# Splitting the first loads of an MLP forward-and-backward kernel, and starting the first product on half of its columns

## The chip, the cores and the metric

The kernel runs on one core of a Trainium2 chip. The metric is device time in microseconds (us) of one execution. A profiled execution's span is about 1.9 us shorter than its time (320.1 against 321.97 us for the kernel before). Times inside a trace count from the start of the span.

## The reference

```python
# x: 2048 x 640, w1: 640 x 1536, w2: 1536 x 640, grad_out: 2048 x 640, all bf16
h   = silu(x @ w1)
out = h @ w2
# returned: out and the gradients of x, w1 and w2 for grad_out
```

## The kernel before

Everything is 128 x 128 weights times up to 512 moving columns on TensorE. Rows of x are handled in four chunks of 512 (four tiles of 128). For each chunk the kernel makes h transposed (`h_group`, 12 groups of 5 matmuls), the output, and the gradients that go back to x; at the end come the two weight gradients. The first chunk of x is transposed on TensorE, since nothing else can run yet; later chunks come transposed by DMA.

The parts that the change touches, with cuts marked:

```python
NWARM = 36
warm = cpool.tile([P, P], dt_in, name="warm")
nc.vector.memset(warm[:], 0.0)
nc.scalar.activation(warm_a[:], warm[:, 0:1], ACT.Silu)      # loads the table early
for i in range(NWARM):                                       # L97: warm-up, result unused
    nc.tensor.matmul(wp[:, 0:P], lhsT=warm[:], rhs=warm[:], start=True, stop=True)
# ... cut
def pe_xT(c, halves):                                        # called as pe_xT(0, 1)
    # ... cut
        for dt_ in range(DT):
            # ... cut: the bank tp is allocated
            for j in range(nst):                             # L125: 4 transposes into one bank (st = j here)
                nc.tensor.transpose(tp[:, j, :], x_nat[:, st, dt_*P:(dt_+1)*P], ident[:])
            # copy the bank to xT: VectorE (L128) for even dt_, ScalarE (L130) for odd

FH = FC // 2                                                 # 256
nc.sync.dma_start(out=x_nat[:, 0:STC, :], in_=x_v[:, 0:STC, :])         # 640 KB
nc.sync.dma_start(out=w1_nat[:, :, 0:FH], in_=w1_v[:, :, 0:FH])         # 320 KB
nc.sync.dma_start(out=w1_nat[:, :, FH:FC], in_=w1_v[:, :, FH:FC])       # 320 KB
# ... cut: rest of w1, w2, transposed loads
xT_next = pe_xT(0, 1)

def h_group(ft, xT, aT, ghT):
    hp = ps_h.tile([P, SC], FP32, name="hp")
    for dt_ in range(DT):                                    # L151: 5 matmuls, 512 columns
        nc.tensor.matmul(hp[:], lhsT=w1_nat[:, dt_, ft*P:(ft+1)*P], rhs=xT[:, dt_, :],
                         start=(dt_ == 0), stop=(dt_ == DT - 1))
    # ... cut: Silu and Tanh on ScalarE, two VectorE instructions

# chunk c, cut:
if c == 1:
    for j in range(0, ST, STC):                              # 4 transfers, used at the very end
        nc.sync.dma_start(out=go_nat[:, j:j + STC, :], in_=go_v[:, j:j + STC, :])
if c == 0:
    for ft in range(FT):
        h_group(ft, xT, aT, ghT)
    # ... cut: store, then sd_phase (L186: output matmuls), ...
```

## Time and profile before

| | before |
|---|---|
| time, median of 3 (of 6 with the comparison runs) | 321.95 us (321.89) |
| span of the profiled execution | 320.1 us |
| x (640 KB) complete | 5.25 us |
| first w1 piece (256 columns) complete | 6.36 us |
| first h matmul | 6.42 us |
| first output matmul | 19.38 us |
| from the start of the last matmul (317.21) to the end ("the tail" below) | 2.90 us |

The two landings are the last of sixteen partial landings: the trace's landing records have sixteen for each of these loads. The chain of waits of the kernel before, its first 21 us (start, duration, what it was):

```profile
0.74 4.51 DMA x_nat<-in_x_dram
5.25 0.05 issue
5.30 1.29 PE tp L125 x20
6.59 12.95 PE hp L151 x60
19.54 1.51 PE hp L186 x7
```

After the load of x there is only TensorE work. The groups view says the same for the whole run (busy us, mean ns; then idle time before them):

```profile
L151 PE MATMUL hp<-xT,w_nat 128*128 128x512 bf16 x240 | 56.9, 379 | 0.0
...
L186 PE MATMUL hp<-aT,w_nat 128*128 128x512 bf16 x240 | 52.5, 379 | 0.0
```

The mean of 379 ns is the length of one pipelined matmul; the pace is 12.95 us for 60, or 216 ns each. The timeline of the kernel before (start, duration, group, count) shows the head:

```profile
0.74 0.43 SPq L134 DMA_DIRECT2D x_nat<-in_x_dram  x1
...
0.99 4.02 PE L97 MATMUL wp<-warm 128*128 128x128 bf16 x36 [0.99 <-DVE warm L92]
...
1.23 0.49 SPq L135 DMA_DIRECT2D w_nat<-in_w_dram  x1
...
5.30 1.29 PE L125 MATMUL tp<-ident,x_nat 128*128 128x128 bf16 x20 [0.28 <-DMA x_nat<-in_x_dram]
...
6.42 13.12 PE L151 MATMUL hp<-xT,w_nat 128*128 128x512 bf16 x60
...
19.38 6.85 PE L186 MATMUL hp<-aT,w_nat 128*128 128x512 bf16 x31
```

How to read a pace here: a group lasts from its first start to its last end. For the warm-up, (4.02 - 0.31) / 35 = 106 ns from start to start; for the transposes, (1.29 - 0.22) / 19 = 56 ns (0.31 and 0.22 us are one instruction's length). Both stream 128 columns: the array ran at half clock in the warm-up and at full clock in the transposes.

### The profile page before, as it was taken

The page shows a single profiled execution, that of the slowest core. Times are in us where ns is not written, and L with a number is a line of the kernel's source. Part 1 is how long each engine was busy: PE and PEld are TensorE (multiplying, and loading weights), DVE is VectorE, ACT ScalarE, POOL GpSimd, SP SyncE. Part 2 cuts the span into 40 slices and gives each one's busy share as a digit, 9 for nine tenths or more (in the row PEclk, how much of TensorE's full clock was granted, in tenths as well). Part 3 has the DMA queues.
Part 4 walks back from the last instruction along what each step waited for, and adds up shares of the span by engine and source line. Part 5 has one row for each costly group of instructions (what it writes and reads, how often), then busy time and mean ns, then how long its engine had stood idle before and what let it go on. Part 6 is the DMA issues. An engine that isn't in the chain of part 4 may idle for free.

```text
span 320.1 us, 3590 instructions
## 1 busy us (share of the span) xinstructions
PE 316.2 (99%) x1512; PEld 146.7 (46%) x1512; DVE 101.9 (32%) x179; ACT 78.3 (24%) x140; POOL 0.7 (0%) x6
## 2 busy tenths in 40 slices
PE   8999999999999999999999999999999999999996
PEld 7444444444444444444444444444444444444443
DVE  1871551477510087710147751000000100001001
ACT  3960001555201255401154520110100001001100
POOL 0000000000000000000000000000000000000000
DMA  8999999999999855291635079809999999994111
GB/s 232 314 194 190 252 222 274 341 263 309 262 286 296 227 180 151 69 324 63 175 109 146 2 247 269 224 16 301 260 241 242 269 209 342 238 293 166 52 37 47
DMA packets 149200, 66.69 MB, mean 208 GB/s; under 512 B 112576, under 2 KB 149184, under 8 KB 149184
## 3 DMA queue, kind: packets, MB, share of 16 engines
q1 hardware_dynamic: 149184, 66.46, 81.8%
q8 instruction: 12, 0.20, 0.3%
q14 instruction: 4, 0.03, 0.0%
HBM read 9.18 MB, written 28.97 MB: 119 GB/s over the span
## 4 chain that ended last, share of the span: by engine, by line
PE 98%; DMA 1%; DVE 0%; issue 0%; DVEq 0%
PE hp L186 32%; PE hp L151 16%; PE hp L276 16%; PE hp L170 16%; PE hp L324 15%; DMA x_nat<-in_x_dram 1%; PE hp L306 1%; PE tp L125 0%; DVE g_2364 L317 0%; DVEq L317 0%
## 5 line engine op out<-in xcount | busy, mean ns | idle before, releaser
L151 PE MATMUL hp<-xT,w_nat 128*128 128x512 bf16 x240 | 56.9, 379 | 0.0
L170 PE MATMUL hp<-goT,w2T 128*128 128x512 bf16 x240 | 56.9, 379 | 0.0
L186 PE MATMUL hp<-aT,w_nat 128*128 128x512 bf16 x240 | 52.5, 379 | 0.0
L186 PE MATMUL hp<-ghT,w1T 128*128 128x512 bf16 x240 | 52.5, 379 | 0.0
L276 PE MATMUL hp<-a_blk,go_nat 128*128 128x512 bf16 x240 | 52.0, 379 | 0.0
L324 PE MATMUL hp<-gh_blk,x_nat 128*128 128x512 bf16 x224 | 48.5, 379 | 0.0
L194 ACT ACTIVATE oT<-hp 128x512 bf16<-128x512 f32 x24 | 14.3, 597 | 110.0 <-PE hp L186 110.0
L186 PEld LDWEIGHTS <-w_nat 128*128 128x128 bf16 x240 | 23.5, 98 | 28.3
L170 PEld LDWEIGHTS <-w2T 128*128 128x128 bf16 x240 | 23.5, 98 | 28.3
L276 PEld LDWEIGHTS <-go_nat 128*128 128x128 bf16 x240 | 23.5, 98 | 28.3
L186 PEld LDWEIGHTS <-w1T 128*128 128x128 bf16 x240 | 23.4, 98 | 28.4
L158 ACT ACTIVATE aT<-hp 128x512 bf16<-128x512 f32 x48 | 28.7, 598 | 31.1 <-PE hp L151 31.1
L151 PEld LDWEIGHTS <-w_nat 128*128 128x128 bf16 x240 | 23.4, 98 | 28.1
L196 DVE CAST oT<-hp 128x512 bf16<-128x512 f32 x16 | 11.1, 692 | 78.0 <-PE hp L186 78.0
L177 DVE SCALAR_TENSOR_TENSOR ghT<-ghT,hp 128x512 bf16<-128x512 bf16 x48 | 32.5, 683 | 7.3 <-PE hp L170 7.3
L324 PEld LDWEIGHTS <-x_nat 128*128 128x128 bf16 x224 | 21.9, 98 | 26.4
L163 DVE SCALAR_TENSOR_TENSOR ghT<-aT,v 128x512 bf16<-128x512 bf16 x48 | 33.0, 688 | 0.6
L162 DVE TENSOR_SCALAR v<-t 128x512 bf16<-128x512 f32 x48 | 20.5, 427 | 28.5 <-ACT t L160 28.5
L160 ACT ACTIVATE t<-hp 128x512 f32<-128x512 f32 x48 | 28.4, 591 | 0.0
L286 DVE CAST g2T<-hp 128x512 bf16<-128x512 f32 x7 | 4.8, 692 | 46.1 <-PE hp L276 46.1
L284 ACT ACTIVATE g2T<-hp 128x512 bf16<-128x512 f32 x8 | 4.8, 598 | 47.0 <-PE hp L276 47.0
L97 PE MATMUL wp<-warm 128*128 128x128 bf16 x36 | 4.0, 313 | 1.0 <-DVE warm L92 1.0
(32 smaller groups left out, 27.0 us busy)
## 6 DMA issues: line engine op xcount, KB each, us to landing
aT_scr<-aT SPq DMA_DIRECT2D x4, 1536.0 KB, 6.2
ghT_scr<-ghT SPq DMA_DIRECT2D x4, 1536.0 KB, 10.1
out_dram<-o_sb SPq DMA_DIRECT2D x8, 640.0 KB, 3.4
x_nat<-in_x_dram SPq DMA_DIRECT2D x4, 640.0 KB, 4.7
oT_scr<-oT SPq DMA_DIRECT2D x4, 640.0 KB, 4.3
go_nat<-in_grad_out_dram SPq DMA_DIRECT2D x4, 640.0 KB, 7.1
gxT_scr<-oT SPq DMA_DIRECT2D x4, 640.0 KB, 4.7
w_nat<-in_w_dram SPq DMA_DIRECT2D x2, 960.0 KB, 11.3
```

What stands on the lines that cost most here:

```text
L151: nc.tensor.matmul(hp[:], lhsT=w1_nat[:, dt_, ft * P:(ft + 1) * P], rhs=xT[:, dt_, :], start=(dt_ == 0), stop=(dt_ == DT - 1),)
L158: nc.scalar.activation(aT[:, ft, :], hp[:], ACT.Silu)
L160: nc.scalar.activation(t[:], hp[:], ACT.Tanh, scale=0.5)
L162: nc.vector.tensor_scalar(out=v[:], in0=t[:], scalar1=-0.5, scalar2=0.5, op0=ALU.mult, op1=ALU.add)
L163: nc.vector.scalar_tensor_tensor(out=ghT[:, ft, :], in0=aT[:, ft, :], scalar=1.0, in1=v[:], op0=ALU.subtract, op1=ALU.mult)
L170: nc.tensor.matmul(gp[:], lhsT=w2T[:, dt_, ft * P:(ft + 1) * P], rhs=goT[:, dt_, :], start=(dt_ == 0), stop=(dt_ == DT - 1),)
L177: nc.vector.scalar_tensor_tensor(out=ghT[:, ft, :], in0=ghT[:, ft, :], scalar=1.0, in1=gp[:], op0=ALU.add, op1=ALU.mult)
L186: nc.tensor.matmul(op_[:], lhsT=w_all[:, ft, dt_ * P:(dt_ + 1) * P], rhs=rhs_all[:, ft, :], start=(ft == 0), stop=(ft == FT - 1),)
L194: nc.scalar.activation(oT[:, dt_, :], op_[:], ACT.Copy)
L196: nc.vector.tensor_copy(out=oT[:, dt_, :], in_=op_[:])
L276: nc.tensor.matmul(gp[:], lhsT=go_nat[:, st, dt_ * P:(dt_ + 1) * P], rhs=a_blk[:, st, :], start=(st == 0), stop=(st == ST - 1),)
L324: nc.tensor.matmul(gp[:], lhsT=x_nat[:, st, dt_ * P:(dt_ + 1) * P], rhs=gh_blk[:, st, :], start=(st == 0), stop=(st == ST - 1),)
```

## The change

The intent: h needs x and w1, and half of the rows of the chunk are enough for a start. So two tiles of x and 256 columns of w1 come first (640 KB instead of 960), the second tile through ScalarE's queue. The first two h groups start on 256 columns; tiles 2 and 3 are transposed between them; then the groups are completed. The warm-up reads a constant and so starts earlier, with fewer matmuls, and four filler matmuls follow the first transposes to keep TensorE busy.

```diff
-    NWARM = 36
+    NWARM = 26
+    NFILL = 4
@@
-        warm = cpool.tile([P, P], dt_in, name="warm")
-        nc.vector.memset(warm[:], 0.0)
+        warm = nc.const_aps.tensor(1.0, (P, P), dt_in)
@@
-        nc.sync.dma_start(out=x_nat[:, 0:STC, :], in_=x_v[:, 0:STC, :])
-        nc.sync.dma_start(out=w1_nat[:, :, 0:FH], in_=w1_v[:, :, 0:FH])
-        nc.sync.dma_start(out=w1_nat[:, :, FH:FC], in_=w1_v[:, :, FH:FC])
+        load_x_tile(nc.sync, 0)
+        load_x_tile(nc.scalar, 1)
+        load_w1(0, FH)
+        load_x_tile(nc.sync, 2)
+        load_x_tile(nc.sync, 3)
+        load_w1(FH, FC)
 ... (ScalarE's early Silu moves behind its load)
-        xT_next = pe_xT(0, 1)
+        def pe_x_tile(xT, st):        # 3 transposes, VectorE copy; 2 transposes, ScalarE copy
+            ...
+        for st in range(2):
+            pe_x_tile(xT_next, st)
+        for i in range(NFILL):
+            nc.tensor.matmul(wp[:, 0:P], lhsT=ident[:], rhs=x_nat[:, 1, 0:P], start=True, stop=True)
 ... (h_mm: the five matmuls of a group on columns lo to hi)
             if c == 0:
-                for ft in range(FT):
+                hps = []
+                for ft in range(2):
+                    hp = ps_h.tile([P, SC], FP32, name="hp")
+                    h_mm(hp, ft, xT, 0, XL)          # XL = 256
+                    hps.append(hp)
+                    pe_x_tile(xT, 2 + ft)
+                for ft in range(2):
+                    h_mm(hps[ft], ft, xT, XL, SC)
+                    h_group(ft, xT, aT, ghT, hps[ft])
+                for ft in range(2, FT):
                     h_group(ft, xT, aT, ghT)
```

More of the change, by code (lines that the diff above doesn't have):

```diff
@@ L89 @@
         opool = mctx.enter_context(tc.tile_pool(name="opool", bufs=2))
-        warm = cpool.tile([P, P], dt_in, name="warm")
-        nc.vector.memset(warm[:], 0.0)
+        warm = nc.const_aps.tensor(1.0, (P, P), dt_in)
         warm_a = cpool.tile([P, 1], FP32, name="warm_a")
-        nc.scalar.activation(warm_a[:], warm[:, 0:1], ACT.Silu)
         wp = ps_h.tile([P, SC], FP32, name="wp", tag="hp")
         for i in range(NWARM):
-            nc.tensor.matmul(wp[:, 0:P], lhsT=warm[:], rhs=warm[:], start=True, stop=True)
+            nc.tensor.matmul(wp[:, 0:P], lhsT=warm, rhs=warm, start=True, stop=True)
         ident = cpool.tile([P, P], dt_in, name="ident")
@@ L115, in load_goT, with load_w1, load_x_tile @@
             return goT
-        def pe_xT(c, halves):
-            xT = xpool.tile([P, DT, SC], dt_in, name="xT")
-            nst = STC // halves
-            for hh in range(halves):
-                for dt_ in range(DT):
-                    tp = ps_h.tile([P, nst, P], dt_in, name="tp", tag="hp")
-                    for j in range(nst):
-                        st = c * STC + hh * nst + j
-                        nc.tensor.transpose(tp[:, j, :], x_nat[:, st, dt_ * P:(dt_ + 1) * P], ident[:])
-                    dst = xT[:, dt_, hh * nst * P:(hh + 1) * nst * P]
-                    if dt_ % 2 == 0:
-                        nc.vector.tensor_copy(out=dst, in_=tp[:].rearrange("p j q -> p (j q)"))
-                    else:
-                        nc.scalar.copy(out=dst, in_=tp[:].rearrange("p j q -> p (j q)"))
-            return xT
-        FH = FC // 2
-        nc.sync.dma_start(out=x_nat[:, 0:STC, :], in_=x_v[:, 0:STC, :])
-        nc.sync.dma_start(out=w1_nat[:, :, 0:FH], in_=w1_v[:, :, 0:FH])
-        nc.sync.dma_start(out=w1_nat[:, :, FH:FC], in_=w1_v[:, :, FH:FC])
+        FH = FC // 2
+        XL = SC // 2
+        xT_next = xpool.tile([P, DT, SC], dt_in, name="xT")
+        def load_w1(lo, hi):
+            nc.sync.dma_start(out=w1_nat[:, :, lo:hi], in_=w1_v[:, :, lo:hi])
+        def load_x_tile(eng, st):
+            eng.dma_start(out=x_nat[:, st, :], in_=x_v[:, st, :])
+        load_x_tile(nc.sync, 0)
[4 more added lines that the diff above has]
+        load_w1(FH, FC)
         for fc in range(1, NFC):
-            nc.sync.dma_start(out=w1_nat[:, :, fc * FC:(fc + 1) * FC], in_=w1_v[:, :, fc * FC:(fc + 1) * FC])
+            load_w1(fc * FC, (fc + 1) * FC)
+        nc.scalar.activation(warm_a[:], warm[:, 0:1], ACT.Silu)
         for hf in range(2):
@@ L144, with h_mm @@
         nc.sync.dma_start_transpose(out=w1T[:], in_=w1[:, :])
-        xT_next = pe_xT(0, 1)
-        def h_group(ft, xT, aT, ghT):
-            hp = ps_h.tile([P, SC], FP32, name="hp")
+        DS = 3
+        def pe_x_tile(xT, st):
+            for lo, hi, copy in ((0, DS, nc.vector.tensor_copy), (DS, DT, nc.scalar.copy)):
+                tp = ps_h.tile([P, hi - lo, P], dt_in, name="tp", tag="hp")
+                for dt_ in range(lo, hi):
+                    nc.tensor.transpose(tp[:, dt_ - lo, :], x_nat[:, st, dt_ * P:(dt_ + 1) * P], ident[:])
+                copy(out=xT[:, lo:hi, st * P:(st + 1) * P], in_=tp[:])
+        for st in range(2):
+            pe_x_tile(xT_next, st)
+        for i in range(NFILL):
+            nc.tensor.matmul(
+                wp[:, 0:P], lhsT=ident[:], rhs=x_nat[:, 1, 0:P], start=True, stop=True
+            )
+        def h_mm(hp, ft, xT, lo, hi):
             for dt_ in range(DT):
                 nc.tensor.matmul(
-                    hp[:],
+                    hp[:, lo:hi],
                     lhsT=w1_nat[:, dt_, ft * P:(ft + 1) * P],
-                    rhs=xT[:, dt_, :],
+                    rhs=xT[:, dt_, lo:hi],
                     start=(dt_ == 0),
@@ L157, in h_group @@
                 )
+        def h_group(ft, xT, aT, ghT, hp=None):
+            if hp is None:
+                hp = ps_h.tile([P, SC], FP32, name="hp")
+                h_mm(hp, ft, xT, 0, SC)
             nc.scalar.activation(aT[:, ft, :], hp[:], ACT.Silu)
@@ L216 @@
             if c == 0:
-                for ft in range(FT):
+                hps = []
+                for ft in range(2):
+                    hp = ps_h.tile([P, SC], FP32, name="hp")
+                    h_mm(hp, ft, xT, 0, XL)
[5 more added lines that the diff above has]
+                for ft in range(2, FT):
                     h_group(ft, xT, aT, ghT)
```

## The prediction

> **What bounds the kernel now.** The chain of waits is TensorE matmuls for 98% of the 320.1 us span. Only its head is anything else: 4.51 us from the issue of the x load (0.74) until its last part lands (5.25), then 20 transposes (1.29 us). From 6.4 us on TensorE never idles (groups: idle 0.0 for the big matmul lines; 60 matmuls take 12.95 us, 216 ns each). So only the first 6.4 us can be shortened, and what is saved there should reach the end undiminished.
>
> In the DMA landings x (640 KB) is complete at 5.25, the first 256 columns of w1 (320 KB) at 6.36, the next 256 at 7.45. The first h matmul starts at 6.42: transposes and w1 piece end together, so both have to move.
>
> **What changes.**
> 1. Before the first h matmul 640 KB must land instead of 960. In the DMA records 655,000 bytes had moved by 4.36 us, 983,000 by 5.30; landings trailed by 0.9 to 1.0 us. Estimate: x tiles 0 and 1 land at 4.0 to 4.4, the w1 piece at 5.2. The second issuing queue saves little: the Trainium skill ("DMA: Bandwidth & Descriptors", Issuing engines are not separate DMA queues) says both run on the same 16 engines. The first h matmul then starts near 5.2, 1.2 us earlier.
> 2. Given back: ten transposes now come after that start (10 x 56 ns = 0.56 us). Half-width matmuls cost nearly nothing more (0.03 us). And a new wait: the upper halves need the copies of tile 3. The old first copy began 0.43 us after the first transpose and took 0.43; with three transposes and 384 columns I estimate 0.77 from first transpose to first upper-half matmul, of which transposes fill 0.29: a stall of about 0.48 us. Sum: about 1.1 us.
> 3. Net: 0.1 to 0.2 us earlier at the output matmuls, which started at 19.38.
>
> Not critical: later loads (w1 columns 256 to 511 needed near 8.4, landing about 7.4), activations (first Silu near 8.2 instead of 7.71; the twelfth result is needed only 2.4 us into the output matmuls).
>
> 4. Clock. Warm-up matmuls are 106 ns apart until 4.7, transposes from 5.30 on 56 ns: the clock doubled between. The Trainium skill ("TensorE: Matmul & The Clock Gate", Part 1) puts this at about 4 us of sustained activity, judged in a free-running window of 3.4 us. The new warm-up starts 0.25 us earlier, but 26 matmuls run out near 3.5; a gap, short transposes and four fillers follow. Most likely the clock is up by 5.2; if it comes a window later, 3.4 us of h at half rate cost up to 1.7 us. I give that 1 in 5.
>
> **Prediction: 321.7 us**, 0.25 under the 321.95 measured; range 320.9 to 322.7. Chances: faster by over 2% 0.01, within 2% 0.98, slower 0.01.
>
> **What would show each step right or wrong** (new profile): first h matmul near 5.2, released by the landing of the w1 piece; transposes of tiles 2 and 3 not waiting for DMA; an idle of about 0.5 us before the first upper-half matmul, released by the VectorE copy; first half-width matmuls about 110 ns apart (215 if the clock is down); output matmuls starting at 19.2 to 19.3; no idle afterwards.
>
> **What would make it wrong.** The w1 piece landing by 4.8 (if the slow first microsecond of the x load, about 120 GB/s against 330 to 400 later, is a limit of one queue that two lift) would gain another 0.4; a late clock would turn the gain into a loss near 1.5; x tiles 2 or 3 landing after 5.8 and 6.6 would stall the interleaved transposes.

## More of the kernel before

One more view mattered, and I had not looked at it before predicting: what SyncE's queue waits for in the last 5 us (total us, times, longest).

```profile
SPq L363 <- DMA out_dram<-g_2364: 0.5, 1, 0.5
...
SPq L363 <- DMA out_dram<-g_2344: 0.3, 1, 0.3
```

The last two stores are waited for one after the other, g_2364 being the very last.

## The result, and the profile after

| | before | after |
|---|---|---|
| time, median of 6 | 321.89 us (321.7 to 322.4) | 322.5 us (322.1 to 323.04) |
| span of the profiled execution | 320.1 | 321.1 |
| tiles 0 and 1 of x complete | 5.25 (all four) | 3.62 and 3.80 |
| first w1 piece complete | 6.36 | 6.04 (15 of 16 parts by 4.94) |
| first h matmul | 6.42 | 6.08 |
| first output matmul | 19.38 | 20.13 |
| last matmul's start to the end (the tail) | 2.90 | 3.18 |

The ratio is 1.0018, 95% interval 1.0004 to 1.0032: same at 2%, and slower by a fifth of a per cent.

The chain of waits after, first 21 us:

```profile
0.74 0.39 SPq L124
...
1.19 4.84 DMA w_nat<-in_w_dram
...
6.08 0.72 PE hp L160 x5
6.80 0.28 PE tp L148 x5
7.08 0.55 PE hp L160 x5
7.63 0.18 PE tp L148 x3
...
7.83 0.37 DVE xT L149
...
8.25 1.47 PE hp L160 x11
```

Left out are stretches of 0.02 to 0.06 us of "issue". The load that ends last is now w1's, and a VectorE copy (7.83) has entered the chain. The timeline after:

```profile
0.74 0.40 ACTq L124 DMA_DIRECT2D x_nat<-in_x_dram  x1
...
1.19 0.41 SPq L121 DMA_DIRECT2D w_nat<-in_w_dram  x1
...
3.67 1.25 PE L148 MATMUL tp<-ident,x_nat 128*128 128x128 bf16 x10
...
4.71 0.58 PE L154 MATMUL wp<-x_nat,ident 128*128 128x128 bf16 x4
...
6.08 0.72 PE L160 MATMUL hp<-xT,w_nat 128*128 128x256 bf16 x5 [0.80 <-DMA w_nat<-in_w_dram]
...
6.64 0.44 PE L148 MATMUL tp<-ident,x_nat 128*128 128x128 bf16 x5
...
7.47 0.44 PE L148 MATMUL tp<-ident,x_nat 128*128 128x128 bf16 x5
...
8.25 12.04 PE L160 MATMUL hp<-xT,w_nat 128*128 128x256 bf16 x59 [0.34 <-DVE xT L149]
...
20.13 6.21 PE L200 MATMUL hp<-aT,w_nat 128*128 128x512 bf16 x27
```

The last transpose of tile 3 started at 7.69 and the next matmul at 8.25, where 56 ns would have done: a stall of 0.50 us. The fillers are still 106 ns apart (half clock, until 5.03); the transposes at 6.64 are 56 ns apart. From first h matmul to first output matmul it is 14.04 us (20.126 - 6.084 in the records), against 12.95 before (19.376 - 6.423): 1.09 us given back. And at the end, SyncE's queue waits:

```profile
SPq L386 <- DMA out_dram<-g_2375: 1.1, 1, 1.1
```

Only one store is waited for now, the very last one, and for all of the time.

### The profile page after: what moved, and what is told of

It reads as the page before. It is cut to its first block, busy times and chain, and to the rows that moved or that the text cites. A ratio compares the mean times of both kernels' runs of the same rounds, so it can differ in the third digit from the quotient of the medians.

```text
span 321.1 us, 3575 instructions
## 1 busy us (share of the span) xinstructions
PE 314.7 (98%) x1487; PEld 147.5 (46%) x1516; DVE 101.8 (32%) x179; ACT 78.2 (24%) x142; POOL 0.7 (0%) x6
## 3 DMA queue, kind: packets, MB, share of 16 engines
HBM read 9.18 MB, written 28.97 MB: 119 GB/s over the span
## 4 chain that ended last, share of the span: by engine, by line
PE 97%; DMA 2%; issue 1%; DVE 0%; SPq 0%; DVEq 0%
PE hp L200 32%; PE hp L160 16%; PE hp L184 16%; PE hp L299 16%; PE hp L347 15%; DMA w_nat<-in_w_dram 2%; PE hp L329 1%; PE tp L148 0%; SPq L124 0%; DVE xT L149 0%; DVE g_2375 L340 0%; DVEq L340 0%
## 5 line engine op out<-in xcount | busy, mean ns | idle before, releaser
L160 PE MATMUL hp<-xT,w_nat 128*128 128x512 bf16 (+1 forms) x243 | 56.9, 370 | 1.5 <-DMA w_nat<-in_w_dram 0.8
L160 PEld LDWEIGHTS <-w_nat 128*128 128x128 bf16 x250 | 24.4, 98 | 28.5 <-DMA w_nat<-in_w_dram 1.0
L200 PEld LDWEIGHTS <-w_nat 128*128 128x128 bf16 x240 | 23.5, 98 | 28.3
L356 ACT ACTIVATE g_2149<-hp 128x512 bf16<-128x512 f32 x1 | 0.6, 597 | 13.5 <-DMA out_dram<-g_2086 13.5
```

Of the source, the lines that this page charges most:

```text
L160: nc.tensor.matmul(hp[:, lo:hi], lhsT=w1_nat[:, dt_, ft * P:(ft + 1) * P], rhs=xT[:, dt_, lo:hi], start=(dt_ == 0), stop=(dt_ == DT - 1),)
L200: nc.tensor.matmul(op_[:], lhsT=w_all[:, ft, dt_ * P:(dt_ + 1) * P], rhs=rhs_all[:, ft, :], start=(ft == 0), stop=(ft == FT - 1),)
```

## The experiments

The changed kernel's six times fell in two groups (322.1 to 322.2, 322.8 to 323.0), so single traces could mislead. My theory after the first trace was a straggling part of the w1 load (S) against a fixed late landing (F); rivals for the rest were a late clock (C), and for the end another order of final waits (K).

### The changed kernel again

No edit.

> The changed kernel once more, unchanged, for a second trace and five more times. In the first trace of it one of the sixteen landings of the first w1 piece came at 6.04 us, 1.1 us after the fifteenth (4.94), and its six times fell in two groups (322.1 to 322.2 and 322.8 to 323.0). Theory S (a straggling transfer that comes and goes): two groups again; if the profiled run is one of the quick ones, the w1 piece is complete by about 5.0 to 5.3, the first h matmul starts then, and the output matmuls at about 19.1 to 19.4. Rival F (the late landing is a fixed property of the new load order): complete at about 6.0 again, output matmuls at about 20.1, median 322.5 again.

Measured: 322.31 us median (321.94 to 322.49), ratio 1.0013 (1.0001 to 1.0025). In this trace the w1 piece was complete at 4.98, the first h matmul started at 5.03, the first output matmul at 19.07. The timeline:

```profile
3.95 0.73 PE L148 MATMUL tp<-ident,x_nat 128*128 128x128 bf16 x10 [0.30 <-DMA x_nat<-in_x_dram]
4.52 0.39 PE L154 MATMUL wp<-x_nat,ident 128*128 128x128 bf16 x4
5.03 0.72 PE L160 MATMUL hp<-xT,w_nat 128*128 128x256 bf16 x5
...
7.19 2.98 PE L160 MATMUL hp<-xT,w_nat 128*128 128x256 bf16 x18 [0.34 <-DVE xT L149]
```

S holds for this piece, and F falls; but the two groups that I expected did not come back, for the five times (321.94, 322.10, 322.31, 322.47, 322.49) spread without a gap. The way from first h to first output matmul is again 14.04 us, and the tail again 3.17. Note the clock: the same ten transposes and four fillers took 0.73 and 0.39 us here, 1.25 and 0.58 in the first trace. In this execution the clock had doubled by 3.95; in the other it had not by 5.03. Note also that although TensorE ended 0.31 us earlier than in the kernel before, the span is the same 320.1 us.

### One queue

```diff
-        load_x_tile(nc.scalar, 1)
+        load_x_tile(nc.sync, 1)
```

> x tile 1 is issued by SyncE as tile 0 is, so nothing is issued by ScalarE. If the second queue causes the late last landing of the w1 piece (a transfer of one engine pushed behind), the sixteen landings lie within about 0.8 us again, as before the change, the first h matmul starts near 5.3 to 5.5 and the time falls by about 0.6 us against the slow group of the change (322.0 or so). If the second queue helps (it spread the first microsecond's slow transfers over two queues: tiles 0 and 1 landed at 3.6 and 3.8 where I had estimated 4.0 to 4.4), tile 1 lands about 0.4 us later and the w1 piece too, with the straggler still there: 322.5 to 323.

Measured: 322.82 us (322.66 to 322.98), ratio 1.0031 (1.0019 to 1.0043), slower than the change. Two of sixteen parts of the w1 piece straggled (5.95 and 5.97 after 5.09), so the second queue is not what causes stragglers. My second case had tile 1 land about 0.4 us later than with two queues (3.80 in the first trace); it landed earlier, at 3.50, and tile 0 at 2.98 instead of 3.62. So for the tiles of x the second queue was no help; what moved later was the w1 piece behind them. The first 655 KB had moved by 4.68 us, against 4.02 to 4.21 in the traces with two queues. The issues in this kernel's timeline show why:

```profile
0.74 0.87 SPq L124 DMA_DIRECT2D x_nat<-in_x_dram  x2
1.66 0.43 SPq L121 DMA_DIRECT2D w_nat<-in_w_dram  x1
```

Each issue takes about 0.43 us here, 160 KB or 640 KB alike, and w1 stands behind two of them: it is issued at 1.66 instead of 1.19. How much of the longer time comes from this and how much from the two late parts, one trace can't tell.

### Fourteen fillers

```diff
-    NFILL = 4
+    NFILL = 14
```

> 14 fillers instead of 4, so TensorE is busy without a gap until 5.7 to 6.1 us. It shows when the clock doubles (spacing of fillers going from 106 to 56 ns). In the change the spacing was still 106 at 5.03 and 56 at 6.64. If the clock doubles only near 5.5 to 6.1, a w1 piece that landed at 5.0 would have met a cold array, and an early landing would have been worth less than 1.2 us. Time: within 0.4 us of the change if landing and not fillers sets the first h matmul; if the gap in TensorE's work delays the clock in some executions (theory C for the slow group: late clock), this one has no slow group and a median near 322.1.

Measured: 322.84 us (321.84 to 323.27), ratio 1.0022 (1.0007 to 1.0038).

```profile
4.90 1.68 PE L154 MATMUL wp<-x_nat,ident 128*128 128x128 bf16 x14
6.39 0.74 PE L160 MATMUL hp<-xT,w_nat 128*128 128x256 bf16 x5
```

The lines are of this kernel's timeline. All fourteen fillers ran 106 ns apart, (1.68 - 0.31) / 13 with the last one at 6.28, and the clock doubled within the first h matmuls, at about 6.4. The w1 piece had landed at 4.66. Four fillers would have ended near 5.3, so the other ten held h back by about 1.1 us. In this execution work without a pause from 3.85 on did not bring the clock sooner than 6.4, and the two groups did not vanish (321.84 and 322.02, the others from 322.65): the expectation that they would, if gaps delayed the clock, failed.

### The second lower half after tile 3's transposes

```diff
-                    h_mm(hp, ft, xT, 0, XL)
-                    pe_x_tile(xT, 2 + ft)     # for ft = 0, 1
+                h_mm(hps[0], 0, xT, 0, XL)
+                pe_x_tile(xT, 2)
+                pe_x_tile(xT, 3)
+                h_mm(hps[1], 1, xT, 0, XL)
```

> The second lower-half group comes after the transposes of tile 3 instead of before those of tile 2, so that tile 3's copies run beside it. In the change TensorE stood still from the last transpose of tile 3 (7.69, 56 ns) to the first upper-half matmul (8.25): 0.50 us. If that stall is a real cost on the critical path, it falls to about 0 and the time by 0.4 to 0.5 us against the change (ratio to before near 1.000, from 1.0018). If tiles 2 or 3 then arrive too late (tile 3 landed at 6.97 where it would be wanted 0.85 us after the first h matmul), part of it turns into a wait for their load. Time from the first h matmul to the first output matmul: 13.55 us instead of 14.05.

Measured: 321.76 us (321.21 to 322.36), ratio 1.0000 (0.9988 to 1.0012). In the trace the stall is gone (last transpose at 6.827, next h matmul at 6.883), and 0.19 us of waiting for tile 3's load have come. The first half group met a half-speed array (197 and 213 ns between half-width matmuls instead of 108); from first h to first output matmul it is 13.93 us, about 13.5 without these two, where I expected 13.55. The median is 0.55 us under that of the unchanged change in the same batch; the intervals overlap, so the trace, not the time, is the firm part.

### The number of transfers, in the changed kernel

```diff
-                for j in range(0, ST, STC):
-                    nc.sync.dma_start(out=go_nat[:, j:j + STC, :], in_=go_v[:, j:j + STC, :])
+                nc.sync.dma_start(out=go_nat[:, :, :], in_=go_v[:, :, :])
```

> The changed kernel with grad_out's rows loaded by one transfer instead of four, in a stage where nothing waits for them (issued about 55 us into the run, needed after 213 us). That brings the number of transfers back to that of the kernel before. From the start of the last matmul to the end the kernel before took 2.90 us and all five traces with the new load order 3.17: SyncE's waits at the end stand in another order, the wait for the last store first (1.12 us) and four satisfied waits of 65 ns each after it. Theory K (the count of transfers decides which wait is last): the tail is 2.90 us again and the time 0.27 us lower, ratio near 1.0006 to 1.001. Rival (the tail comes from something else in the change): 3.17 us, and ratio near 1.0015.

Measured: tail 2.91 us, as theory K has it; time 322.29 us (322.01 to 322.44), ratio 1.0016 (1.0002 to 1.0029). So the tail is settled and the time did not show it: the head of these executions differed by as much. SyncE's queue waits, in this kernel's waits view, for two stores again:

```profile
SPq L385 <- DMA out_dram<-g: 0.9, 2, 0.5
```

### The number of transfers, in the kernel before

```diff
-                for j in range(0, ST, STC):
-                    nc.sync.dma_start(out=go_nat[:, j:j + STC, :], in_=go_v[:, j:j + STC, :])
+                for lo, hi in ((0, 1), (1, 2), (2, 3), (3, 4), (4, 8), (8, 12), (12, 16)):
+                    nc.sync.dma_start(out=go_nat[:, lo:hi, :], in_=go_v[:, lo:hi, :])
```

> The kernel before, with grad_out's rows loaded by seven transfers instead of four: three transfers more, as the change has. Theory K: its tail grows from 2.90 to 3.17 us and the time by 0.27 us, ratio near 1.0008. Rival: 2.90 us and 1.000. Its head is the old one, so it is a second trace of it: w1's first piece complete at about 6.2 to 6.5, first h matmul 6.4 to 6.5, at full clock; the transposes from 5.3 on may be at half clock if the clock doubles late in this execution, which would then cost up to 1.1 us (20 transposes at 106 instead of 56 ns).

Measured: 322.29 us (322.03 to 322.73), ratio 1.0016 (1.0004 to 1.0029); tail 3.15 us. K holds both ways for the tail. (The mean time rose by more than the tail, 0.47 us over the kernel before in the batch; the rest is not explained by the edit.) In the trace's semaphore instructions, counted from the start of the last matmul:

```
                         first wait ends  second   third   fourth  fifth   end
before                   1.04             1.11     1.17    1.54    2.11    2.90
after                    2.13             2.19     2.26    2.33    2.39    3.18
after, 1 transfer less   1.04             2.10     2.17    2.23    2.29    3.08
after, grad_out in one   1.04             1.11     1.17    1.53    2.12    2.91
before, 3 more           2.10             2.17     2.24    2.30    2.36    3.15
```

(The third row is the single-transfer kernel below.) The wait for the last store ends at about 2.1 us in all of them. If its wait stands first, four waits of about 65 ns each follow it; if it stands last, they are done in its shadow. The change has three transfers more than before, and that moved it to the front; with one transfer less than that it stands second.

This trace of the old head also has a late clock: its transposes ran at half clock until 6.59, and h began at 6.92 instead of 6.42 although w1 had landed at 6.22. Two lines of its timeline:

```profile
5.12 1.97 PE L125 MATMUL tp<-ident,x_nat 128*128 128x128 bf16 x20
6.92 2.75 PE L151 MATMUL hp<-xT,w_nat 128*128 128x512 bf16 x12
```

### No fillers

```diff
-    NFILL = 4
+    NFILL = 0
```

> No fillers. In the four traces so far the four fillers ended at 4.75 us (clock already doubled) or at 5.0 to 5.4 (not yet). Where the w1 piece has landed by then (4.66, 4.79) the fillers hold the first h matmul back by up to 0.4 us. If fillers do keep the clock up or bring it sooner (their intent), leaving them out costs time: first half-width h matmuls about 215 ns apart in more executions, median above 322.5. If the clock's doubling is set by something else (its moment differed from 3.5 to 6.4 us between executions of the same warm-up), leaving them out gains 0 to 0.3 us: 322.0 to 322.4.

Measured: 322.38 us (322.12 to 322.85), ratio 1.0019 (1.0006 to 1.0032): no different from the change, so four fillers neither help nor harm measurably. The trace has another straggler, in the second w1 piece (columns 256 to 511): last part at 8.61, about 1.9 us after the eighth. Lines of its chain of waits:

```profile
2.72 5.89 DMA w_nat<-in_w_dram
8.61 0.05 issue
8.65 3.41 PE hp L160 x15
```

### Everything together

No fillers, grad_out in one transfer, and a third step that works on tile 2's columns while tile 3 is copied:

```diff
-                for ft in range(2):
-                    h_mm(hps[ft], ft, xT, XL, SC)
-                    h_group(ft, xT, aT, ghT, hps[ft])
+                for ft in range(2):
+                    h_mm(hps[ft], ft, xT, XL, XL + P)
+                for ft in range(2):
+                    h_mm(hps[ft], ft, xT, XL + P, SC)
+                    h_group(ft, xT, aT, ghT, hps[ft])
```

> The version that the runs point to: no fillers; the columns of tile 2 used as a third step (two half groups of 128 columns) while tile 3 is copied, so that neither the stall of 0.50 us nor a wait for tile 3's load (0.19 us in the reordered kernel) is left; and grad_out in one transfer. If the three costs add up (stall 0.50, tail 0.27, fillers about 0.1 on average): 0.8 to 0.9 us under the change, 321.5, ratio to before 0.999 to 0.9995, single executions from 321.0. From first h matmul to first output matmul 13.6 us at full clock.

Measured: 321.59 us (321.43 to 321.94) against 321.75 of the kernel before in the same batch, ratio 0.9994 (0.9981 to 1.0007). About 0.7 us under the median of the repeated change (322.31, another batch), but not shown to beat the kernel before. From first h to first output matmul it took 14.03 us, not the 13.6 that I expected. A wait for tile 2's load (landed at 5.82) had taken the stall's place, as this kernel's timeline shows:

```profile
4.86 0.72 PE L160 MATMUL hp<-xT,w_nat 128*128 128x256 bf16 x5 [0.40 <-DMA w_nat<-in_w_dram]
5.86 0.45 PE L148 MATMUL tp<-ident,x_nat 128*128 128x128 bf16 x5 [0.28 <-DMA x_nat<-in_x_dram]
```

### Four warm-up matmuls

```diff
-    NWARM = 26
+    NWARM = 4
```

> The changed kernel with 4 warm-up matmuls instead of 26, so that TensorE has almost no work until the tiles of x land at 3.6 us. In ten traces the clock doubled 2.8 to 5.7 us after the first warm-up matmul, spread over about 3 us without regard to the kernel. If TensorE's own activity starts that count (theory C: the clock is a term of the sum), it now doubles at about 6.4 to 9.3, and each us after 5.2 costs half a us: 1.0 us more than the change on average, about 323.3, ratio near 1.005, with a wide spread of single times. If the moment does not depend on the warm-up at all, the time stays at 322.3 to 322.5.

Measured: 323.42 us (322.71 to 323.85), ratio 1.004 (1.0027 to 1.0053). The clock doubled between 8.63 and 9.18. So it came 7.9 to 8.4 us after the first warm-up matmul, later than in all thirteen traces with more warm-up (2.6 to 5.9). Theory C holds in this: with less work before it the full clock comes later, and a late clock is paid for. What exactly starts the count, one trace does not show. From its timeline:

```profile
5.56 1.26 PE L160 MATMUL hp<-xT,w_nat 128*128 128x256 bf16 x5
6.61 0.74 PE L148 MATMUL tp<-ident,x_nat 128*128 128x128 bf16 x5
7.14 1.27 PE L160 MATMUL hp<-xT,w_nat 128*128 128x256 bf16 x5
```

The half groups take 1.26 instead of 0.72 us. The way to the first output matmul is 21.06 - 5.56 = 15.5 us instead of 14.04.

### Both lower halves first

As "everything together", but tiles 2 and 3 are transposed after both lower half groups.

```diff
                 for ft in range(2):
                     hp = ps_h.tile([P, SC], FP32, name="hp")
                     h_mm(hp, ft, xT, 0, XL)
                     hps.append(hp)
-                    pe_x_tile(xT, 2 + ft)
+                for ft in range(2):
+                    pe_x_tile(xT, 2 + ft)
```

> As the combined version before it, but with both lower half groups ahead of the transposes of tiles 2 and 3. There TensorE waited 0.45 us for the load of tile 2 (wanted at 5.41, landed at 5.82); here it has 0.55 us of matmuls to do first, and tile 3 is wanted 0.3 us later still. If that wait was the largest thing left, 0.2 to 0.4 us less than the combined version: 321.2 to 321.4, ratio 0.9985. A small wait for the copies of tile 2 (about 0.15 us) may appear.

Measured: 321.86 us (321.45 to 322.23) against 322.13 of the kernel before in this batch, ratio 0.9991 (0.9978 to 1.0004). No wait for a load of x is left after the first h matmul, but this profiled execution had a late clock (half-width matmuls up to 213 ns apart, full clock from about 6.6), and copies of tile 2 were waited for (0.2 us). My 321.2 to 321.4 was too low. The two combined versions lie 0.06% and 0.09% under the kernel before, with intervals that include 1: unclear.

### The constant warm-up alone, in the kernel before

```diff
-        warm = cpool.tile([P, P], dt_in, name="warm")
-        nc.vector.memset(warm[:], 0.0)
+        warm = nc.const_aps.tensor(1.0, (P, P), dt_in)
```

(and 38 warm-up matmuls instead of 36)

> One part of the change alone in the kernel before: the warm-up reads the constant of ones instead of a tile that VectorE clears first, so it starts at about 0.75 instead of 0.99, with 38 matmuls instead of 36 to end at the same time. As the h matmuls wait until 6.4 for w1 in any case, I expect no change: 321.6 to 321.9, ratio 1.0000. Tail 2.90 us (same count of transfers). It is a third trace of the old head: clock doubling anywhere from 3.5 to 6.5; when after 5.3 it costs the transposes up to 0.5 us.

Measured: 321.85 us (321.68 to 322.22), ratio 0.9995 (0.9983 to 1.0007): no effect, as expected. Clock doubled at 6.06, h from 6.68.

### Two tiles in one transfer

```diff
-        load_x_tile(nc.sync, 0)
-        load_x_tile(nc.scalar, 1)
+        nc.sync.dma_start(out=x_nat[:, 0:2, :], in_=x_v[:, 0:2, :])
```

> Tiles 0 and 1 of x in one transfer by SyncE, nothing issued by ScalarE. With one queue and two transfers the w1 piece was issued at 1.66 instead of 1.19 (each issue takes about 0.43 us whatever its size) and its data moved about 0.5 us later (655 KB by 4.68 instead of 4.02 to 4.21). Theory I (issue time): one transfer puts the w1 issue back to 1.19, 655 KB have moved by 4.1 to 4.3, the w1 piece lands near 4.9 (stragglers apart), and the time is as in the change or up to 0.1 us less. Rival Q (two queues feed the engines faster): 655 KB by about 4.4 to 4.7, as with the one large load of the kernel before (4.33 to 4.36), landing at 5.2 or later, time 0.2 to 0.5 us over the change.

Measured: 322.45 us (321.93 to 322.83), ratio 1.0011 (0.9999 to 1.0023). With one queue, the w1 piece was issued at 1.25, 655 KB had moved by 4.21, and the piece landed at 5.08. That fits theory I: what ScalarE's queue saved was, in the main, one issue of SyncE. (4.21 is as late as the latest of the two-queue traces, so a further gain of up to 0.2 us from two queues is not excluded by this one trace, and the time does not decide it.) The array was slow until 6.7, in this kernel's timeline:

```profile
5.12 0.63 PE L153 MATMUL wp<-x_nat,ident 128*128 128x128 bf16 x4
5.56 1.26 PE L159 MATMUL hp<-xT,w_nat 128*128 128x256 bf16 x5
```

## Why the prediction was right or wrong

The time, 322.5 us, lies in the stated range of 320.9 to 322.7, and "within 2%" was right. The direction was wrong: I put 0.25 us of gain at the centre (my own sum gave only 0.1 to 0.2), and the medians differ by 0.6 us the other way. That the time lay in the range all the same is partly luck: the errors below have opposite signs, and the range was wide. What failed is step 3, the net gain at the output matmuls (predicted 19.2 to 19.3; 20.13 and 19.07 in the two traces of the changed kernel), through stragglers that had no term and a clock whose odds I had too favourable, and with it the claim that a gain there reaches the end. Point by point:

- **What bounds the kernel** was right. TensorE ran without a wait from the first output matmul to the last matmul: 297.83 us from one start to the other in both first traces (317.21 - 19.38 and 317.96 - 20.13), and in all twelve others. So what the head gains or loses arrives in full at the last matmul. It does not at the end of the kernel; see the tail.
- **"Given back: about 1.1 us"** was right to a few hundredths: 14.04 - 12.95 = 1.09 us, with a stall of 0.50 us before the first upper half where I had 0.48, released by the VectorE copy as said. The reordered kernel removed it.
- **"The w1 piece at 5.2"** was pessimistic for most executions and optimistic for some. With the two-queue loads it landed at 4.66 to 4.99 in eight of nine traces and at 6.04 in the ninth. With them the first two tiles of x came at 3.5 to 4.0 rather than 4.0 to 4.4. The reason I gave for expecting little of the second queue, the Trainium skill's statement ("DMA: Bandwidth & Descriptors", Issuing engines are not separate DMA queues) that both queues run on the same 16 engines, so that only the issuing sequencer's time is saved, agrees with the single-transfer kernel (655 KB by 4.21 us with one queue). What I did not do was cost that time: one issue is 0.43 us, and it stands directly ahead of the critical load.
- **Stragglers** were not in my sum. In three traces of the old load order the last part of each of the first five loads came 0.18 to 0.49 us after the eighth part. In ten of eleven traces of the new order at least one of the first five was worse than that, up to 1.6 us, and in the eleventh the sixth load was 1.94 us late. The old order is not free of them: in one of its three traces the sixth load was 1.65 us late, where nothing waited for it. Since h now starts closer behind its loads, such a part is waited for (6.04 in the first trace; 8.61 in the kernel without fillers). It is no matter of the second queue, since both one-queue kernels have it too. Why the first loads of the new order spread more is not settled; no run isolates it.
- **"Most likely the clock is up by 5.2 ... I give that 1 in 5"** was mis-sized in its odds and in its cost. In thirteen traces with 26 or more warm-up matmuls the doubling came anywhere from below 4 to 6.7 us, and in four of the ten with the changed warm-up length h began on an array still at half clock (in a fifth, only its fillers kept h back until then). The cost is smaller than my estimate of up to 1.7 us, because the doubling comes by 6.7: 0.5 us more for five half-width matmuls at 213 ns, and 0.4 to 0.55 us for transposes and fillers that end later (h at 5.56 in the single-transfer kernel, whose w1 piece had landed at 5.08, and at 5.39 in the reordered kernel, where it had landed at 4.79; as an estimate they would have started 0.05 us after the landing, as in the second trace of the change, 5.03 after 4.98). The old head pays too (h at 6.92 and 6.68 instead of 6.42). That a late clock costs time is shown by the kernel with four warm-up matmuls.
- **"What is saved there should reach the end undiminished"** failed at the very end. The tail of 2.90 us became 3.18 because three more transfers moved the wait for the last store ahead of four satisfied waits. This 0.27 us (3.17 to 3.18 against 2.90) was in none of my terms. Taking the transfers away from the changed kernel or adding them to the old one switched it off and on.

As a sum: all 11 executions of the changed kernel average 322.41 us, 37 of the kernel before 321.93, so 0.48 us slower, with a standard error of 0.12. Of this 0.27 is the tail, which I had as zero. By subtraction the head is then about 0.2 us slower, where I had 0.1 to 0.2 faster. Two runs bear on that, by the mean times of their batch: the changed kernel without its longer tail (grad_out in one transfer) was still 0.40 us above the kernel before (standard error 0.10), and the kernel before with a longer tail (seven transfers) was 0.47 above (0.15), of which the tail explains 0.25. So a slower head is likely, and its size is not settled. The earlier landing (0.2 to 0.5 better than I assumed) must then have been outweighed. The traces show two things that can do it, each worth up to about 1 us at the first output matmul: a straggler (20.13 in the first trace against 19.07 in the second) and a late clock (20.14 in the single-transfer kernel). How they share the difference is not resolved: each trace is one execution, and times of one kernel scatter by as much.

## What to carry to other kernels

When only the first microseconds can be shortened, list what else is set by them or by the program's shape: when the array's clock comes up, how long each DMA issue takes ahead of the critical load, the last of sixteen partial landings rather than the typical one, and the order of the waits at the end. Put independent work behind every small copy that the next matmul needs: one half group placed after the transposes instead of before them removed a 0.5 us stall. A change of less than 0.2% can't be judged by one trace, since one execution's clock and stragglers are as large as the effect: compare stage starts over several traces, and times over many executions.

## What the Trainium skill lacked or had wrong

- "TensorE: Matmul & The Clock Gate", Part 1, says the transition happens around 4 us into sustained activity, within 500 ns from run to run. Counted from the first warm-up matmul, it came here after 2.6 to 3.2 us in one trace (the changed kernel again: still half at 3.39, doubled before 3.95, start 0.77) and after 5.9 us in another (two tiles in one transfer: 6.7, start 0.77). In the late traces TensorE had paused for 0.3 to 0.6 us between warm-up and transposes, so that their activity was not quite sustained; the one trace that doubled with no pause before (one queue) did so after 3.8 us, as the page has it. Its account of a free-running window of 3413 ns fits that spread better than its 500 ns; no run shows the window itself. The profile's granted clock does not show this half speed: it reads 1.00 in the first 4 us, where matmuls of 128 columns were 106 ns apart.
- The same page, Part 4, says that full clock does not engage for transposes. Here transposes were 56 ns apart at full clock and 106 ns at half clock. (The profile lists them as MATMUL and does not show whether a transpose mode was on.)
- "DMA: Bandwidth & Descriptors", Issuing engines are not separate DMA queues, calls the saved issue time usually small relative to the DMA. So it is here, but not small for a head of 6 us: one issue took about 0.43 us for 160 KB and 640 KB alike, against 2.9 us from the issue of tile 0 of x to its landing (0.74 to 3.62), and one issue more in front moved the data of the next load by about 0.5 us (655 KB by 4.68 instead of 4.02 to 4.21).
- No page that I read gives how far the sixteen parts of one load land apart: 0.2 to 0.5 us from the eighth to the last in the first five loads with the old order (1.65 in the sixth of one trace), up to 1.6 in the first five with the new one (1.94 in a sixth).
- No page that I read says that the kernel's end waits for each store semaphore in turn, about 65 ns each, in an order that the number of transfers decides: 0.27 us here.
